# Two kinds of elementwise instruction of the attention stage moved to GpSimd

## The chip, the cores and the metric

One core of one Trainium2 chip. The time is the device time of one execution in microseconds (us), the median of three runs. Engines are called as in the profile: PE (TensorE matmul), PEld (TensorE weight load), DVE (VectorE), ACT (ScalarE), POOL (GpSimd), SP (SyncE, which issues most of the transfers here).

## What is computed

Three layers, one after another, all in float32; batch 4, 448 tokens, 12 heads of 64, model width 768:

```
attn  = sigmoid(q @ k.T / 8 - log(448)) @ v                  # per head
h     = relu(x @ w_in)                                       # 768 -> 1024, u and v are its halves
gated = u * (w_spatial @ layernorm(v) + b_spatial)
x     = gated @ w_out                                        # 512 -> 768
theta = x @ w_theta                                          # 768 -> 768
u     = x + w_tok_r @ (x * cos(theta)) + w_tok_i @ (x * sin(theta))
out   = u + relu(u @ w_ch)
```

The weights arrive as 64-bit floats and are brought to float32 on the chip.

## The kernel before

Most products are made of three passes: each operand is split into a high part (rounded to the 32-bit form that TensorE takes in one pass, `F32R`) and a low part (operand minus high part), and PE adds up high x high, high x low and low x high. So each operand needs one copy, which makes the high part, and one subtraction, which makes the low part. Both lie on DVE and ACT, beside PE.

The change touches the first of the stages, attention together with the product by `w_in`. The 48 heads (4 x 12) are worked as 24 pairs, numbered n = 0 to 23, and the pairs as 12 rounds of two. Its order is written by hand for PE, ACT, DVE and SP (`tc.manual_schedule`); POOL isn't on that list, so a planner places its instructions. A round r does this:

- `end_scores(nxt)`: scores of the 64 last tokens of the next round's pairs (tile `pse`), and their sigmoid on ACT.
- `begin_pieces(1)`, `end_pieces()`: steps of the weight pipeline, described below.
- `begin_attend` and `attend(cur)`: the products with v of this round's pairs (tile `psa`); ACT copies each result out of PSUM as the high part of `X` and DVE subtracts (`L56` in the profile, `X<-psa,X`), which frees the PSUM buffer. DVE also copies 64 columns to `XL`.
- `scores(t, g)` for both pairs of the next round, three `pss` tiles each, with a sigmoid on ACT for each (`af<-pss`).
- more steps of the weight pipeline, with `split_pair` of the two pairs of the round after that: DVE makes the high part of keys and queries (`kqh`, a cast of 128x896) and the low part (`kql`, a subtraction of 128x896).
- `uv`: products of finished heads with `w_in` (tile `psd`). There is none in rounds 0 to 2; round 3 has the first three.

All the PSUM tiles of this stage (`pse`, `psa`, `pss`, `psd`) rotate through four buffers of one tag. The third `pss` of a round takes the buffer of the round's first `psa`, the fourth that of the second: these matmuls start when DVE is through with the subtraction `X<-psa,X`.

The weight pipeline takes `w_in` in 12 pieces of 128x512 (class `Piece`), and behind them the pieces of other weights, which are only brought to float32 and stored. A piece passes through: load (SP), `low` (DVE, two instructions, L99 and L101), `high` (ACT, L106), `join` (DVE, L111, which makes the float32 value `q`), `part_high` (ACT, the high part `wih<-wq`), and `part_low` (DVE, the low part `wil<-wq,wih`). `begin_pieces` issues `part_low` of the pieces joined last time, then `join`, then `low` of the next ones, then loads; `end_pieces` issues `part_high` of the pieces just joined and `high` of the next ones. Between `join` and `part_low` of one piece there is one half of a round. From 30 to 55 us, two or three pieces pass in a round.

Pair 0 has no split: its scores are computed in plain float32. Pair 1 is split ahead of round 0, pairs 2 and 3 too, and rounds 0 to 3 split pairs 4 and 5, 6 and 7, 8 and 9, 10 and 11.

Of the kernel before, what the change touches and what calls it, by code (L numbers as in the profile page):

```python
# [14 lines left out]
ALU = mybir.AluOpType  # L15
# [35 lines left out]
def net(ctx: ExitStack, tc: tile.TileContext, kq, vd, vl, w_in, w_sp, bsp, w_out, w_th, w_tok, w_ch, out):  # L51
    nc = tc.nc
    ve, se, te = nc.vector, nc.scalar, nc.tensor

    def sub(o, a, b):
        ve.tensor_tensor(out=o, in0=a, in1=b, op=ALU.subtract)  # L56
# [4 lines left out]
    def acopy(o, a, f=AF.Copy):  # L61
        se.activation(o, a, f)  # L62
# [84 lines left out]
    wih = wi_p.tile([P, KC, DFF], F32R, name="wih")  # L147
# [29 lines left out]
    def split_pair(t):  # L177
        r = t["r"]
        hi = t["h"] = at.tile([P, 2, S], F32R, tag="kqh", name="kqh", bufs=NKQ)
        lo = t["l"] = at.tile([P, 2, S], F32R, tag="kql", name="kql", bufs=NKQ)  # L180
        ve.tensor_copy(hi, r)
        sub(lo, r, hi)

    def sigmoid(tag, ps, bufs):
        af = at.tile([P, 2, S], F32, tag=tag, name="af", bufs=bufs)
# [77 lines left out]
    class Piece:  # L263
# [18 lines left out]

        def part_high(self):
            if self.dst is None:
                acopy(wih[:, self.k, self.s], self.q)

        def part_low(self):
            if self.dst is None:
# [58 lines left out]
    with tc.manual_schedule(engines={mybir.EngineType.PE, mybir.EngineType.Activation, mybir.EngineType.DVE, mybir.EngineType.SP}):  # L347
# [4 lines left out]
        for t in rounds[0] + rounds[1]:  # L352
            load_v(t)
        split_pair(rounds[0][1])
        for g in range(3):
            scores(rounds[0][0], g)
        ae = end_scores(rounds[0])
        rounds[2] = [load_kq(4 + i) for i in range(2)]
        for t in rounds[1]:
            split_pair(t)  # L360
        for g in range(3):
            scores(rounds[0][1], g)
        for r in range(R):
# [24 lines left out]
            if aft:  # L388
                split_pair(aft[0])
# [96 lines left out]
    for i in range(2):  # L486
        t = pa.tile([P, DH], F32R, name=f"vb{i}", bufs=1)
# [452 lines left out]
```

## Time and profile before

| | us |
|---|---|
| three runs | 630.32, 624.97, 627.34; median 627.34 |
| profiled execution | 626.07 |
| its span in the trace | 624.3 |
| PE busy | 612.6 (98%) |
| PEld, DVE, ACT, POOL busy | 507.1, 415.8, 346.9, 23.8 |
| granted TensorE clock | full speed in all 40 slices |

The median of the three runs lies 1.27 us above the profiled execution. Matmuls are pipelined and their ends are modelled, so a PE that is shown as busy can still be waiting; whether it waits is read from the chain of waits and from the starts of its matmuls.

### The profile page before, as it was taken

The numbers are of one execution on the slowest core, as the hardware profiler recorded it, in microseconds if no ns is written. First come the engines' busy times: TensorE is split into PE (matmuls) and PEld (weight loads), VectorE is DVE, ScalarE is ACT, GpSimd is POOL, SyncE is SP. The second block draws the span as 40 slices with busy tenths as digits, with TensorE's granted clock in tenths as the row PEclk, the third lists the DMA queues.
The fourth block names the chain that finished last, engine by engine and source line by source line (L and its number), as shares of the span: only waits on it lengthen the run. The fifth ranks groups of instructions, "written<-read, shape, count | busy, mean of one in ns | idle before, by whom it ended". The sixth has DMA issues, their size and how long they took to land.

```text
span 624.3 us, 9178 instructions
## 1 busy us (share of the span) xinstructions
PE 612.6 (98%) x3296; PEld 507.1 (81%) x3296; DVE 415.8 (67%) x798; ACT 346.9 (56%) x588; POOL 23.8 (4%) x42
## 2 busy tenths in 40 slices
PE   6999999999999999999999999999999999899997
PEld 2455667757776688999999999999999999789996
DVE  3899576627663559794231386797776797688875
ACT  5799466564555425274336486666567566362540
POOL 0000000000000100100000000101101101000000
PEclk9999999999999999999999999999999999999999
DMA  8787588857864685865767612464183123354603
GB/s 308 239 266 233 187 237 277 271 170 250 291 212 144 203 287 180 245 207 181 220 198 230 161 39 65 89 215 114 56 247 92 50 102 126 113 191 134 224 29 134
DMA packets 82675, 112.63 MB, mean 180 GB/s; under 512 B 27842, under 2 KB 69188, under 8 KB 82628
## 3 DMA queue, kind: packets, MB, share of 16 engines
q1 hardware_dynamic: 74820, 99.18, 50.6%
q10 hardware_dynamic: 7808, 12.85, 5.9%
q8 instruction: 26, 0.43, 0.3%
q14 instruction: 21, 0.17, 0.1%
HBM read 68.06 MB, written 32.93 MB: 162 GB/s over the span
## 4 chain that ended last, share of the span: by engine, by line
PE 79%; DVE 11%; DMA 4%; ACT 3%; issue 2%; SPq 0%; POOL 0%; ACTq 0%; POOLq 0%; DVEq 0%
PE psa L224 7%; PE pss L199 6%; PE psd L65 3%; PE psd L243 3%; PE ppo L66 3%; PE ppo L67 3%; PE ppo L65 3%; PE psd L66 3%; PE psd L67 3%; PE psd L245 3%; PE psd L244 3%; PE pt L638 3%; PE pt L639 3%; PE pt L637 3%; PE py L678 3%; PE py L679 3%
## 5 line engine op out<-in xcount | busy, mean ns | idle before, releaser
L186 ACT ACTIVATE af<-pss,bias 128x896 f32<-128x896 f32 x72 | 66.1, 1020 | 2.8 <-PE pss L199 2.8
L637 PE MATMUL pt<-thh,XT 128*128 128x384 f32 x168 | 56.9, 338 | 0.3 <-DVE r L644 0.3
L638 PE MATMUL pt<-thl,XT 128*128 128x384 f32 x168 | 56.9, 338 | 0.0
L224 PE MATMUL psa<-af,vr 128*64 128x448 f32 x288 | 56.8, 543 | 0.0
L639 PE MATMUL pt<-thh,XT 128*128 128x384 f32 x168 | 56.8, 338 | 0.0
L224 PEld LDWEIGHTS psa<-af,vr 128*64 128x64 f32 x288 | 19.6, 137 | 36.3 <-issue 35.2
L62 ACT ACTIVATE ev<-psd 128x448 f32<-128x448 f32 (+1 forms) x30 | 17.0, 568 | 52.5 <-PE psd L67 26.0
L111 DVE SCALAR_TENSOR_TENSOR wq<-wraw,wq 128x384 int32<-128x384 int32 (+2 forms) x51 | 28.7, 594 | 23.7 <-ACT wraw L106 23.6
L65 PE MATMUL psd<-X,wih 128*128 128x448 f32 x96 | 35.6, 371 | 0.0
L106 ACT ACTIVATE wraw<-wraw 128x384 f32<-128x384 f32 (+2 forms) x51 | 29.6, 604 | 10.7 <-DVE wq L99 7.4
L66 PE MATMUL ppo<-g,wbh 128*128 128x448 f32 x96 | 35.2, 366 | 0.0
L67 PE MATMUL ppo<-g,wbl 128*128 128x448 f32 x96 | 35.1, 366 | 0.0
L65 PE MATMUL ppo<-g,wbh 128*128 128x448 f32 x96 | 35.1, 366 | 0.0
L67 PE MATMUL psd<-X,wil 128*128 128x448 f32 x96 | 35.1, 365 | 0.0
L66 PE MATMUL psd<-X,wih 128*128 128x448 f32 x96 | 35.1, 365 | 0.0
L56 DVE TENSOR_TENSOR X<-psa,X 128x448 fp32r<-128x448 f32 x24 | 15.0, 624 | 27.8 <-ACT X L62 27.8
L648 ACT ACTIVATE m<-r 128x384 f32<-128x384 f32 x28 | 14.6, 520 | 32.5 <-DVE r L646 32.5
L637 PEld LDWEIGHTS pt<-thh,XT 128*128 128x128 f32 x168 | 31.5, 188 | 1.1 <-DVE r L644 0.7
L638 PEld LDWEIGHTS pt<-thl,XT 128*128 128x128 f32 x168 | 31.6, 188 | 0.4
L101 DVE SCALAR_TENSOR_TENSOR wq<-wraw,wq 128x384 int32<-128x384 int32 (+2 forms) x51 | 30.6, 600 | 1.8
L639 PEld LDWEIGHTS pt<-thh,XT 128*128 128x128 f32 x168 | 31.5, 188 | 0.0
L62 ACT ACTIVATE xr<-xp 128x768 uint16<-128x768 uint16 x28 | 28.4, 1066 | 0.5 <-ACT x L62 0.5
(287 smaller groups left out, 1583.9 us busy)
## 6 DMA issues: line engine op xcount, KB each, us to landing
kqr<-in_kq SPq DMA_DIRECT2D x24, 448.0 KB, 4.6
wraw<-in_w_in SPq DMA_DIRECT2D x12, 512.0 KB, 5.3
x_d<-x ACTq DMA_DIRECT2D x24, 224.0 KB, 3.3
xb<-x_d SPq DMA_DIRECT2D x4, 1344.0 KB, 7.7
xp<-xa SPq DMA_DIRECT2D x56, 96.0 KB, 2.5
y_d<-y SPq DMA_DIRECT2D x24, 224.0 KB, 2.1
out_t<-o SPq DMA_DIRECT2D x24, 224.0 KB, 2.0
vr<-in_vd SPq DMA_DIRECT2D x24, 192.0 KB, 4.5
```

Of the source, the lines that this page charges most:

```text
L62: se.activation(o, a, f)
L65: te.matmul(ps, wh, xh, start=first, stop=False)
L66: te.matmul(ps, wh, xl, start=False, stop=False)
L67: te.matmul(ps, wl, xh, start=False, stop=last)
L101: ve.scalar_tensor_tensor(out=self.q, in0=self.hi, scalar=-(2 ** 31), in1=self.q, op0=ALU.bitwise_and, op1=ALU.bitwise_or)
L106: se.activation(self.lo.bitcast(F32), self.hi.bitcast(F32), AF.Copy, scale=2.0 ** -112)
L186: se.activation(af, ps[:, :, :S], AF.Sigmoid, bias=bias, scale=1.0 / math.sqrt(D))
L199: te.matmul(ps[:, j, :S], t[w][a, 0, c], t[x][a, 1, :], start=n == 0, stop=n == 2)
L224: te.matmul(ps[a, :S], t["v"][:, 2 * c + j, :], t["a"][c][:, j, :], start=False, stop=c == 2)
L637: te.matmul(o, t[:, k, 0, :], thh[:, k, hs], start=k == 0, stop=False)
L638: te.matmul(o, t[:, k, 0, :], thl[:, k, hs], start=False, stop=False)
L639: te.matmul(o, t[:, k, 1, :], thh[:, k, hs], start=False, stop=k == KC - 1)
```

## The change

Two instructions go to another engine. Nothing else differs; operands, tiles and sizes stay the same.

- `split_pair`: the subtraction that makes the low part of keys and queries is issued on POOL for even n up to 10, which are pairs 2, 4, 6, 8 and 10. For odd n, and from pair 12 on, it stays on DVE.
- `part_high`: the copy that makes the high part of a piece of `w_in` is issued on POOL rather than ACT. That is all 12 pieces.

```
@@ split_pair
         ve.tensor_copy(hi, r)
-        sub(lo, r, hi)
+        (ve if t["n"] % 2 or t["n"] > 10 else nc.gpsimd).tensor_tensor(out=lo, in0=r, in1=hi, op=ALU.subtract)
@@ Piece
         def part_high(self):
             if self.dst is None:
-                acopy(wih[:, self.k, self.s], self.q)
+                nc.gpsimd.tensor_copy(wih[:, self.k, self.s], self.q)
```

## Rows read from the trace of the kernel before

**Rows 1.** Busy time by stretch; us from the start, then each engine's.
```profile
20.00:40.00 20.00, 20.00 (x142) 10.31 (x144) 18.14 (x31) 18.68 (x26) 0.00 (x0) 1.00 0.74 227
40.00:60.00 20.00, 19.80 (x135) 11.00 (x132) 18.57 (x34) 18.28 (x26) 0.00 (x0) 1.00 0.79 261
60.00:80.00 20.00, 20.00 (x119) 13.47 (x119) 12.89 (x25) 11.14 (x19) 0.00 (x0) 1.00 0.56 175
```

**Rows 2.** Chain that ended last, 28 to 58 us: start, length, what.
```profile
31.72 0.64 DVE X L56
...
53.28 0.69 ACT wraw L106
53.98 0.44 ACT X L62
...
54.44 0.64 DVE X L56
...
55.12 2.88 PE pss L199 x24
57.99 0.43 PE psd L243
```

**Rows 3.** Timeline of PE: start, length, instruction, count, [idle before <-who ended it].
```profile
46.96 1.87 PE L217 MATMUL psa<-af,vends 64*64 64x448 f32 x8
...
55.12 0.47 PE L199 MATMUL pss<-kqh 64*128 64x448 f32 x2 [0.20 <-DVE X L56]
```

**Rows 4.** Timeline of DVE, 29 to 60 us.
```profile
29.19 0.69 DVE L101 SCALAR_TENSOR_TENSOR wq<-wraw,wq 128x512 int32<-128x512 int32 x1
30.52 0.62 DVE L56 TENSOR_TENSOR X<-psa,X 128x448 fp32r<-128x448 f32 x1 [0.64 <-ACT X L62]
31.72 0.62 DVE L56 TENSOR_TENSOR X<-psa,X 128x448 fp32r<-128x448 f32 x1 [0.31 <-ACT X L62]
...
37.11 1.09 DVE L56 TENSOR_TENSOR kql<-kqr,kqh 128x896 fp32r<-128x896 f32 x1
38.12 0.68 DVE L56 TENSOR_TENSOR wil<-wq,wih 128x512 fp32r<-128x512 f32 x1
...
47.24 1.09 DVE L56 TENSOR_TENSOR kql<-kqr,kqh 128x896 fp32r<-128x896 f32 x1
48.25 0.62 DVE L181 CAST kqh<-kqr 128x896 fp32r<-128x896 f32 x1
49.91 1.28 DVE L56 TENSOR_TENSOR wil<-wq,wih 128x512 fp32r<-128x512 f32 x2
```

**Rows 5.** Timeline of ACT, 18 to 60 us: the copies that move.
```profile
26.18 1.18 ACT L62 ACTIVATE wih<-wq 128x512 fp32r<-128x512 f32 x2
28.85 0.63 ACT L62 ACTIVATE wih<-wq 128x512 fp32r<-128x512 f32 x1
37.36 0.67 ACT L62 ACTIVATE wih<-wq 128x512 fp32r<-128x512 f32 x1
...
51.83 0.63 ACT L62 ACTIVATE wih<-wq 128x512 fp32r<-128x512 f32 x1 [0.63 <-DVE wq L111]
```

**Rows 6.** POOL and DVE side by side, near 500 and 527 us.
```profile
499.86 1.28 POOL L744 TENSOR_TENSOR wq<-wq 128x192 f32<-128x192 f32 x2 [8.87 <-DVE wcl L56]
500.59 0.96 DVE L627 TENSOR_TENSOR r<-xr,r 128x384 f32<-128x384 f32 x1 [0.60 <-ACT r L649]
501.47 0.54 DVE L627 TENSOR_TENSOR m<-xr,m 128x384 f32<-128x384 f32 x1
...
527.17 0.78 DVE L643 TENSOR_SCALAR m<-m 128x384 f32<-128x384 f32 x1
```

**Rows 7.** DVE's tensor_scalar of that line with POOL idle, near 488 us.
```profile
488.24 0.36 DVE L643 TENSOR_SCALAR m<-m 128x384 f32<-128x384 f32 x1
```

**Rows 8.** POOL's groups: busy, mean ns.
```profile
L488 POOL MEMSET vb<- 64x512 f32 x2 | 1.0, 524 | 201.1 <-PE pss L199 201.1
```

**Rows 9.** Who waited for whom, 60 to 80 us: total, times, longest.
```profile
DVE X L56 <- ACT X L62: 4.9, 2, 3.6
```

More of the change, by code (lines that the diff above doesn't have):

```diff
@@ L181, in split_pair @@
         ve.tensor_copy(hi, r)
-        sub(lo, r, hi)
+        (ve if t["n"] % 2 or t["n"] > 10 else nc.gpsimd).tensor_tensor(out=lo, in0=r, in1=hi, op=ALU.subtract)
     def sigmoid(tag, ps, bufs):
@@ L284, in part_high @@
             if self.dst is None:
-                acopy(wih[:, self.k, self.s], self.q)
+                nc.gpsimd.tensor_copy(wih[:, self.k, self.s], self.q)
         def part_low(self):
```

## The prediction

> **What bounds the kernel now.** I read the busy shares by stretch first. From 20 to 60 us PE, DVE and ACT are all nearly full: of every 20 us DVE works 18.1 and 18.6, ACT 18.7 and 18.3 [rows 1]. From 60 us on, when `uv` comes in, DVE falls to 12.9 and ACT to 11.1 while PE stays full [rows 1]. So the change takes work from two engines that matter only from about 20 to 55 us, which is rounds 0 to 2 and the head of round 3.
>
> Next I read the chain of waits, because a busy PE may still be waiting. Before 31 us the chain lies on PE; from 31.72 it is on DVE (with a little ACT) as far as 54.44, where it passes through an ACT step L106, the copy of `X`, DVE's subtraction `X<-psa,X`, and then the score matmuls at 55.12 [rows 2]. From there it is PE's again. What the reader is to see: in these 23 us DVE, not PE, sets the pace, and it hands over at the subtraction that frees the PSUM buffer which the third `pss` needs. In PE's timeline that is the one visible wait for DVE: 0.20 us before the matmul at 55.12 [rows 3]. So DVE and PE are almost in step there: a faster DVE gains next to nothing, while a slower DVE delays PE from the first microsecond. After 55 us nothing that PE does waits for this, and PE is busy for 98% of the whole span, so a delay that PE has at 55.12 is carried to the end.
>
> **What the subtraction costs where it goes.** On DVE the low part of a pair takes 1.09 us by itself, but 1.01 us of the queue, from its start at 47.24 to the next start at 48.25 [rows 4]. The trace of before has no instruction of this size on POOL. The nearest is POOL's two-input arithmetic on 128x192 near 500 us: two of them in 1.28 us, 0.64 each [rows 6]. That scales by elements to 896/192 x 0.64 = 2.99 us at most.
>
> More important is what DVE does meanwhile. A two-input DVE instruction of 384 columns that starts inside the second of these POOL instructions takes 0.96 us, and its twin right behind it, with POOL idle, 0.54; a one-input `tensor_scalar` takes 0.78 us beside POOL [rows 6] and 0.36 without [rows 7]. Both lose 0.42 us, at whichever form. So a POOL instruction that reads 192 columns twice stops DVE for about 0.42 us of its 0.64. I take 0.42/192 = 2.2 ns a column: a subtraction of 896 columns stops DVE for 1.9 us. Bounds: nothing (if DVE happens to be at work that POOL doesn't stop), and the full 2.99. The middle is what the rows show. Each moved subtraction gives DVE 1.01 us and takes 1.9: net **+0.9 us of DVE time**, not a relief.
>
> **What the copy costs where it goes.** On ACT a copy of 128x512 takes 0.63 us [rows 5]. On POOL no row shows a copy. Below, its hold on DVE is nothing; above, it is that of a two-input instruction, 512 x 2.2 ns = 1.1 us. It reads one operand rather than two, so I take half, 0.55 us; that POOL writes 512 columns in 0.52 us [rows 8] speaks for that order. DVE had nothing of this work before, so each copy is **+0.55 us of DVE time**, where its neighbours on DVE are instructions that POOL stops.
>
> The Trainium skill, "GPSIMD Engine Reference", section "Performance versus the Vector engine", has a two-input add of 2048 columns at 4497 ns against 2293 on VectorE, and its section on when to use GPSIMD puts one-input work at roughly line rate and names VectorE for elementwise work: by estimate 1.97 us for the subtraction and 0.43 us for the copy. With these the sum below would be 5.3 us, so the page speaks against the change as the rows do.
>
> **What ACT gets back.** 12 copies. From 30 to 55 us ACT's step that releases the late `X` is L106 at 53.28, which stands behind DVE's L99, and the copy at 51.83 was itself waiting for DVE (0.63 us) [rows 2, 5]. Its freed time turns into longer waits for DVE. I cost the relief at nothing; at most it is the 0.20 us wait of PE [rows 3] and a second one of under 0.1 behind it.
>
> **The sum.** *Round 0.* DVE is full until 29.88 us (29.19 + 0.69) and then idle for 0.64 before the first `X` subtraction at 30.52 [rows 4]. It gets one pair (pair 4, +0.9) and three copies (two at 26.18, one at 28.85 [rows 5]: 3 x 0.55 = 1.65): 2.55 us. The 0.64 idle covers part, so the first `X` subtraction starts 1.9 late, at 32.4; with the `XL` copy it takes some 0.8 of the queue, so the second starts at 33.2 instead of 31.72: **+1.5**. *Rounds 1 and 2*, 31.72 to 54.44: pairs 6 and 8, 2 x 0.9, and five copies (37.36 to 51.83 [rows 5]), 5 x 0.55: **+4.6**. The third `pss` of round 3 thus starts about 1.5 + 4.6 = 6.1 us later, at 61.2 rather than 55.12. PE's own stalls on the way, such as the 1.87 us that the `psa` matmuls at 46.96 take [rows 3], are on a PE that has to wait for DVE anyway, and give nothing back.
>
> The other moved instructions cost nothing. Pair 2 is split before 16 us with the first PE use at about 20. Pair 10 and the last four copies (0.9 + 4 x 0.55 = 3.1 us) fall after 57 us, where DVE is idle 7.1 of 20 us [rows 1] and waits 4.9 us for `X` [rows 9]. Nothing stands behind them on POOL until its memset after 201 us [rows 8]; no transfer is moved.
>
> One new wait: `wil` on DVE now needs POOL's copy, and behind `wil` stand all the later pieces and the next `X`. Between the `wil` at 38.12 and the next at 43.7 or 49.91 there is half a round, and two copies and a subtraction (1.1 + 1.9 us) fit. If the planner puts the subtraction first, `wil` at 49.91 [rows 4] waits up to half a microsecond; that is inside the range.
>
> Against the profiled execution, 626.07 + 6.1 = 632.2. The median lies 1.27 above it: **633.4 us**, +1.0%.
>
> **Rivals.** *Not slower: POOL works beside DVE.* Then each pair gives DVE 1.01 us back, and PE's last wait, 0.3 us with its successor, goes; what is late next is the sigmoid on ACT, which the change doesn't touch. 626.9 us. It needs DVE and POOL to overlap, against both rows of group 6. Decided at the `X` subtraction of 54.44: earlier or later.
> *Only the subtractions hold DVE*, because a copy reads one operand. Round 0 then adds 0.9 against 0.64 idle and the second `X` is in time; rounds 1 and 2 add 1.8: 629.1 us. No row speaks against it; the `tensor_scalar` in rows 6 and 7, one-input on DVE's side, was held all the same.
> *The hold is dearer*: a copy as dear per column as a subtraction (1.1 us). Round 0: 0.9 + 3.3 - 0.64 - 0.34 = 3.2; rounds 1 and 2: 1.8 + 5.5 = 7.3; 10.5 in all, 637.8 us. The same happens if the hold lasts for all of POOL's 0.64 rather than 0.42. The Trainium skill, "SBUF — State Buffer", section "Who interferes with whom", states that the loser of the pair of ports is blocked for the whole instruction. The 0.42 of 0.64 speaks for part of it, though DVE started some 0.1 us into the second POOL instruction.
>
> **How the numbers follow.** About 1% is what a measurement of this kernel can tell from no change. Chances: forecast 0.52, with its own range 632 to 636 (copies at 0.45 to 0.8 us); no hold 0.12; subtractions only 0.14; dearer 0.22. The 1% line is at 633.6, inside the forecast: half of it, 0.26, falls on either side. Slower by over 1%: 0.26 + 0.22 = 0.48. Within 1%: 0.26 + 0.12 + 0.14, less 0.02 = 0.50. Faster 0.02: nothing in the stretch is worth 6 us. Range 626.5 to 639.
>
> **What would show it.** On POOL, five subtractions of about 2 us and twelve copies of 0.6 to 0.8 us before 80 us; DVE instructions of 20 to 60 us lengthened by 0.5 to 1.9 us each when beside them; the matmuls at 55.12 now near 61, their wait for `X<-psa,X` much above 0.20; from there to the end the same length as before. I am wrong if DVE's instructions keep their lengths there, or if PE's delay at round 3 is made up or grows later on.

## The result, and the profile after

The changed kernel takes 631.10 us against 627.46 (medians of 12 runs each): ratio 1.0067, 95% interval 1.0046 to 1.0089, which is 2.9 to 5.6 us slower; the quotient of the two medians, 1.0058, lies inside. The forecast was slower by 6.1 us, 633.4 us. The measured time is inside the whole range (626.5 to 639) but below the range that the forecast gave its own case (632 to 636), and as near to the 629.1 us of the rival by which only the subtractions hold DVE. So the time alone doesn't decide between these two; the traces and experiments do. The profiled execution took 631.99 us, its span is 630.1; it lies 0.9 us above its median, while the one of before lay 1.4 below, so the two traces differ by more (5.8 us of span) than the medians (3.6).

Where both traces are compared I count from the second `X` subtraction of round 0 (20.53 us before [rows 4 show the ones after it], 20.27 after), because the first loads land at slightly different times. DVE before (start, length, instruction, count, idle before and what ended it), and below it PE before:

```profile
20.53 0.62 DVE L56 TENSOR_TENSOR X<-psa,X 128x448 fp32r<-128x448 f32 x1 [1.25 <-ACT X L62]
...
22.54 0.42 DVE L99 TENSOR_SCALAR wq<-wraw 128x512 int32<-128x512 uint32 x1
...
23.60 0.62 DVE L181 CAST kqh<-kqr 128x896 fp32r<-128x896 f32 x1
...
25.92 1.09 DVE L56 TENSOR_TENSOR kql<-kqr,kqh 128x896 fp32r<-128x896 f32 x1
26.93 1.29 DVE L56 TENSOR_TENSOR wil<-wq,wih 128x512 fp32r<-128x512 f32 x2
```

```profile
57.92 0.50 PE L243 MATMUL psd<-wih,X 128*128 128x512 f32 x1
```

From the second `X` subtraction of round 0 to the first of round 3 it is 33.91 us before (to 54.44 [rows 2]) and 38.28 after: **+4.4**. To the first product by `w_in` (57.92 before) it is 37.39 and 43.14: **+5.7**. From that product to the end it is 566.4 and 566.7 us: no sign that anything is made up or added there, though this stretch scatters by some 6 us between executions (see the experiments).

The stretches of the changed kernel (columns as in rows 1: after the two of the stretch, PE, PEld, DVE, ACT, POOL busy, then the granted clock, DMA share, GB/s):

```profile
20.00:40.00 20.00, 20.00 (x144) 10.03 (x142) 18.24 (x25) 15.64 (x20) 7.83 (x6) 1.00 0.65 211
40.00:60.00 20.00, 16.23 (x104) 8.87 (x102) 18.34 (x30) 12.60 (x18) 5.52 (x5) 0.90 0.75 233
60.00:80.00 20.00, 20.00 (x106) 14.44 (x106) 15.65 (x23) 10.00 (x14) 5.73 (x5) 0.93 0.50 157
```

Against [rows 1], ACT has three to six us less to do in each stretch to 60 us, and DVE is as busy as before although an instruction a round was taken from it. PE has lost 3.6 us between 40 and 60.

DVE in the changed kernel (same columns):

```profile
20.27 0.62 DVE L56 TENSOR_TENSOR X<-psa,X 128x448 fp32r<-128x448 f32 x1 [0.33 <-ACT X L62]
...
22.27 0.83 DVE L99 TENSOR_SCALAR wq<-wraw 128x512 int32<-128x512 uint32 x1
23.14 0.98 DVE L101 SCALAR_TENSOR_TENSOR wq<-wraw,wq 128x512 int32<-128x512 int32 x1
24.05 1.15 DVE L181 CAST kqh<-kqr 128x896 fp32r<-128x896 f32 x2
25.23 2.87 DVE L182 TENSOR_TENSOR kql<-kqr,kqh 128x896 fp32r<-128x896 f32 x1
28.02 1.28 DVE L56 TENSOR_TENSOR wil<-wq,wih 128x512 fp32r<-128x512 f32 x2
...
30.28 0.98 DVE L101 SCALAR_TENSOR_TENSOR wq<-wraw,wq 128x512 int32<-128x512 int32 x1
31.45 0.62 DVE L56 TENSOR_TENSOR X<-psa,X 128x448 fp32r<-128x448 f32 x1 [0.20 <-ACT X L62]
...
35.35 0.43 DVE L99 TENSOR_SCALAR wq<-wraw 128x512 int32<-128x512 uint32 x1 [1.02 <-DMA wraw<-in_w_in]
...
58.55 0.62 DVE L56 TENSOR_TENSOR X<-psa,X 128x448 fp32r<-128x448 f32 x1 [0.48 <-ACT X L62]
```

What the reader is to see: the subtraction of the odd pair, which stayed on DVE, takes 2.87 us rather than 1.09 [rows 4]. L99 at 22.27 takes 0.83 rather than 0.42, and L101 at 23.14 and 30.28 0.98 rather than 0.69 [rows 4]. And there is a wait for a load of `w_in`, which the kernel before didn't have. POOL in the changed kernel, first the subtraction of pair 2, then the instructions of this stretch:

```profile
12.75 2.08 POOL L182 TENSOR_TENSOR kql<-kqr,kqh 128x896 fp32r<-128x896 f32 x1 [11.86 <-DVE kqh L181]
...
24.80 2.36 POOL L182 TENSOR_TENSOR kql<-kqr,kqh 128x896 fp32r<-128x896 f32 x1 [1.21 <-PE pse L207]
29.97 0.74 POOL L285 CAST wih<-wq 128x512 fp32r<-128x512 f32 x1 [2.82 <-DVE wq L111]
34.40 0.61 POOL L285 CAST wih<-wq 128x512 fp32r<-128x512 f32 x1 [3.69 <-DMA wraw<-in_w_in]
```

The subtraction at 24.80 ends at 27.16; DVE's own, issued at 25.23, ends at 28.10, its usual 1.09 us after 27.01. So DVE stood until 0.15 us before POOL was done. The copy at 34.40 ran while DVE was idle: 0.61 us is its own length.

PE at the head of round 3 (same columns):

```profile
59.23 0.66 PE L199 MATMUL pss<-kqh 64*128 64x448 f32 x2 [1.93 <-DVE X L56]
59.68 0.58 PE L199 MATMUL pss<-kql,kqh 64*128 64x448 f32 x2
...
63.41 0.50 PE L243 MATMUL psd<-wih,X 128*128 128x512 f32 x1
```

The wait of 0.20 us for `X<-psa,X` [rows 3] has become 1.93. Then the matmuls take 0.58 us rather than about 0.37: the granted clock has fallen (0.90 and 0.93 in these stretches, against 1.00 before), so part of the time is at the lower of the two levels, 1.2 instead of 2.4 GHz. It is there from 45.6 to 49.2 (granted clock 0.53) and from 59.2 to 62.9 (0.54), behind waits of PE of 1.84 and 1.93 us. The third to sixth `pss` of round 3 with what follows take 4.2 us (59.23 to 63.41) rather than 2.8 (55.12 [rows 3] to 57.92): that is the step from +4.4 to +5.7.

The chain of waits shows the new load wait (start, length, what):

```profile
25.23 2.88 DVE kql L182
28.11 0.02 SPq L169
...
28.54 0.02 SPq L90
...
28.58 6.75 DMA wraw<-in_w_in
...
35.35 0.44 DVE wq L99
```

SP issues the loads of keys and queries (L169), which wait until a buffer of `kqr` is free, that is until a low part has been made from it, and behind them on the same queue the piece of `w_in` (L90). In the changed kernel the odd pair's subtraction ends late, so the piece is issued at 28.58. In the timeline of SP of the kernel before the same piece is issued at 27.50 and no DVE instruction waits:

```profile
25.41 1.99 SPq L169 DMA_DIRECT2D kqr<-in_kq  x2
27.50 0.38 SPq L90 DMA_DIRECT2D wraw<-in_w_in  x1
```

### The profile page after: what moved, and what is told of

It reads as the page before. It is cut to its first block, busy times and chain, and to the rows that moved or that the text cites. A ratio compares the mean times of both kernels' runs of the same rounds, so it can differ in the third digit from the quotient of the medians.

```text
span 630.1 us, 9187 instructions
## 1 busy us (share of the span) xinstructions
PE 615.4 (98%) x3296; PEld 509.6 (81%) x3296; DVE 421.2 (67%) x793; ACT 340.5 (54%) x576; POOL 45.6 (7%) x59
## 4 chain that ended last, share of the span: by engine, by line
PE 64%; DVE 14%; DMA 13%; ACT 4%; issue 3%; SPq 1%; POOL 1%; DVEq 0%; ACTq 0%; POOLq 0%
PE psa L224 7%; PE pss L199 5%; PE pt L638 3%; PE pt L639 3%; PE pt L637 3%; PE py L678 3%; PE py L679 3%; PE py L680 3%; DMA v<-v_d 2%; PE psd L65 2%; PE psd L243 2%; DMA wraw<-in_w_in 2%; PE ppo L65 2%; PE ppo L67 2%; PE ppo L66 2%
## 5 line engine op out<-in xcount | busy, mean ns | idle before, releaser
L111 DVE SCALAR_TENSOR_TENSOR wq<-wraw,wq 128x384 int32<-128x384 int32 (+2 forms) x51 | 28.7, 594 | 25.9 <-ACT wraw L106 25.8
L744 POOL TENSOR_TENSOR wq<-wq 128x192 f32<-128x192 f32 x24 | 16.6, 691 | 249.5 <-DMA wq<-f_ch 217.2
L101 DVE SCALAR_TENSOR_TENSOR wq<-wraw,wq 128x384 int32<-128x384 int32 (+2 forms) x51 | 32.6, 639 | 1.8
L637 PEld LDWEIGHTS pt<-thh,XT 128*128 128x128 f32 x168 | 31.5, 188 | 1.3 <-DVE r L644 0.9
L199 PE MATMUL pss<-kqh 64*128 64x448 f32 x138 | 28.6, 411 | 3.8 <-DVE X L56 3.8
```

The source lines that it names most:

```text
L101: ve.scalar_tensor_tensor(out=self.q, in0=self.hi, scalar=-(2 ** 31), in1=self.q, op0=ALU.bitwise_and, op1=ALU.bitwise_or)
L111: ve.scalar_tensor_tensor(out=self.q, in0=self.lo, scalar=3, in1=self.q, op0=ALU.logical_shift_left, op1=ALU.bitwise_or)
L199: te.matmul(ps[:, j, :S], t[w][a, 0, c], t[x][a, 1, :], start=n == 0, stop=n == 2)
L637: te.matmul(o, t[:, k, 0, :], thh[:, k, hs], start=k == 0, stop=False)
```

## The experiments

All are measured beside the kernel before on the same chip, ratios with their 95% intervals. "X of round 3" is the distance defined above, 33.91 us before and 38.28 with the change; it came out within 0.1 us of 33.91 in three kernels that differ from the kernel before only behind it or in writes of POOL, so it is a fine measure of this stretch. The whole span isn't: from the first product by `w_in` to the end the profiled executions took between 565.5 and 571.4 us, without relation to the edit.

**1. Only the subtractions.** The copy is put back on ACT:

```
-                nc.gpsimd.tensor_copy(wih[:, self.k, self.s], self.q)
+                acopy(wih[:, self.k, self.s], self.q)
```

> Only the five subtractions go to POOL; the copies stay on ACT. Theory (POOL's reads stop DVE): the DVE subtraction of the odd pair behind each lasts about 2.87 us rather than 1.09, so each pair costs DVE 1.78 - 1.01 = 0.8 us net; the X subtraction at the head of round 3, at 54.44 before and 58.55 with the whole change, comes at about 55.5 to 56.5, and the ratio is 1.002 to 1.004. Rival (what costs is that the copies arrive late or hold DVE, and the subtractions are relief): the X subtraction is not later than 54.5 and the ratio is 0.998 to 1.001.

Ratio 1.0037 (1.0017 to 1.0057); X of round 3 at 37.49, +3.6, though only 1 to 2 was expected. DVE's odd subtractions take 2.87 or 2.88 us, as expected; the rest is waits for pieces of `w_in`, 1.08, 0.37 and 0.38. One of them:

```profile
22.46 0.43 DVE L99 TENSOR_SCALAR wq<-wraw 128x512 int32<-128x512 uint32 x1 [1.08 <-DMA wraw<-in_w_in]
```

So the hold of the subtractions is shown, and they cost more than their hold, through the loads.

**2. Only the copies.** The subtraction is put back on DVE:

```
-        (ve if t["n"] % 2 or t["n"] > 10 else nc.gpsimd).tensor_tensor(out=lo, in0=r, in1=hi, op=ALU.subtract)
+        sub(lo, r, hi)
```

> Only the twelve copies of w_in go to POOL; the subtractions stay on DVE. Theory (POOL's reads stop DVE): L99 or L101 beside a copy is longer by 0.3 to 0.4 us, eight copies before 55 us add about 2.8 us less the 0.64 us of idle time in round 0, so the X subtraction of round 3 comes at 56 to 57 and the ratio is 1.002 to 1.004. Rival (a copy with one input doesn't hold DVE): 54.0 to 54.5, ratio 1.000 or a little under, since ACT has less to do.

Ratio 1.0044 (1.0020 to 1.0067), which is 1.3 to 4.2 us; X of round 3 at 35.53, +1.6, at the lower end of what was expected. PE waits for it where it waited 0.20 before:

```profile
55.66 0.47 PE L199 MATMUL pss<-kqh 64*128 64x448 f32 x2 [1.83 <-DVE X L56]
```

No load is waited for here. A one-input copy holds DVE as well; the rival that it doesn't is out.

**3. Only what falls behind 57 us.**

```
-        sub(lo, r, hi)
+        (nc.gpsimd if t["n"] == 10 else ve).tensor_tensor(out=lo, in0=r, in1=hi, op=ALU.subtract)
...
-                acopy(wih[:, self.k, self.s], self.q)
+                (nc.gpsimd.tensor_copy if self.s.start == 0 and self.k >= 2 else acopy)(wih[:, self.k, self.s], self.q)
```

> Only what falls behind 57 us goes to POOL: pair 10 and the last four pieces of w_in, where DVE has idle time. Theory (the price is paid only where DVE sets the pace): DVE's instructions beside POOL are longer there too, but PE doesn't wait; ratio 0.999 to 1.001, X subtraction of round 3 at 54.4. Rival (POOL's slower copies delay the products by w_in, or any hold is carried to the end): slower by about a third of the change's cost, ratio 1.002 or more.

Ratio 0.9998 (0.9975 to 1.0021), X of round 3 at 33.87, PE's wait there 0.20 as before. DVE's instructions beside POOL are longer here too (L99 at 57.50 takes 0.83 us, L101 at 58.37 0.98). So the same hold costs nothing that can be measured where DVE doesn't set the pace.

**4. More buffers for keys and queries.** The whole change, with

```
-        r = t["r"] = at.tile([P, 2, S], F32, tag="kqr", name="kqr", bufs=4)
+        r = t["r"] = at.tile([P, 2, S], F32, tag="kqr", name="kqr", bufs=6)
```

> The whole change, with six buffers in place of four for the loaded keys and queries, so that no load of them, nor the piece of w_in queued behind it on SP, waits for a subtraction. Theory (most of the cost is DVE held by POOL; the late load is an addition): DVE's two waits for a piece of w_in (1.02 and 0.34 us) go, the X subtraction of round 3 comes at about 57.2 rather than 58.55, the ratio falls from 1.0067 to about 1.004 to 1.005. Rival (the late loads are the cause): back to 54.5, ratio 1.000 to 1.001. Other rival (the wait only filled time that DVE would have waited anyway): no difference to the change, 1.006 to 1.007.

DVE's waits for `w_in` are gone and X of round 3 is at 37.43, 0.85 us earlier than with the change. The time isn't: 1.0081 (1.0053 to 1.0108), in 6 runs. The expected gain of 1 to 2 us didn't show, and the interval reaches to the change's own ratio and beyond, so this settles only that the late load isn't the main cause. In its profiled execution PE waited 0.99 and 2.62 us and then ran slow score matmuls (0.58 us) too; the granted clock was 0.997 or lower in all 6 executions.

**5. The same work, for nobody.** The kernel before, with POOL's instructions added and their results unused:

```
+    scr = at.tile([P, 2, S], F32, name="scr", bufs=1)
+    scr2 = at.tile([P, DH], F32, name="scr2", bufs=1)
...
         sub(lo, r, hi)
+        t["n"] in (2, 4, 6, 8, 10) and nc.gpsimd.tensor_tensor(out=scr, in0=hi.bitcast(F32), in1=hi.bitcast(F32), op=ALU.subtract)
...
                 acopy(wih[:, self.k, self.s], self.q)
+                nc.gpsimd.tensor_copy(scr2, self.q)
```

> The kernel before, with the same POOL instructions added for nobody: beside each of the five DVE subtractions a subtraction of 128x896 and beside each of the twelve ACT copies a copy of 128x512, written to tiles that nothing reads. Theory (the price is that POOL's reads stop DVE): no relief, so DVE pays 5 x about 1.8 and 0.3 for each copy; the X subtraction of round 3 comes 5 to 7 us later than before when both are counted from the second X subtraction of round 0, more than with the change itself (4.4), ratio 1.007 to 1.011. Rival (the price is that low and high parts come late from POOL): nobody waits for these results, ratio 0.999 to 1.001.

Ratio 1.0114 (1.0082 to 1.0145), X of round 3 at 40.47, +6.6. DVE does what it did before, and one instruction beside each POOL subtraction is 1.5 us longer; L99 and L101 are longer beside the copies, as in the change, and one piece of `w_in` is waited for (0.69 us, in round 0). DVE, then POOL, of this kernel:

```profile
24.69 1.09 DVE L56 TENSOR_TENSOR kql<-kqr,kqh 128x896 fp32r<-128x896 f32 x1
25.70 2.10 DVE L181 CAST kqh<-kqr 128x896 fp32r<-128x896 f32 x1
```

```profile
24.74 2.58 POOL L183 TENSOR_TENSOR scr<-kqh 128x896 f32<-128x896 f32 x1 [1.63 <-DVE kqh L181]
```

Here it is the cast that stands (2.10 rather than 0.62 us [rows 4]); the subtraction that was already running when POOL started is not lengthened, and POOL's own is (2.58, against 2.08 at 12.75 in the changed kernel). The rival, that results from POOL come late, is out as the cause: nobody waits for these.

**6 and 7. POOL that only writes.** Two memsets of 128x896 behind the split of each even pair up to 10. In the first form DVE read one element of the tile ahead of each of the two (in the cuts `tick` takes that element, and `scr` is a list that holds the tile):

```
         sub(lo, r, hi)
+        [(ve.tensor_copy(tick, s[0:1, 0:1]), nc.gpsimd.memset(s, 0.0)) for s in (2 * scr if t["n"] in (2, 4, 6, 8, 10) else ())]
```

> The kernel before, with two POOL memsets of 128x896 (about 1 us each, no reads) behind the cast of each even pair up to 10, into a tile of which DVE reads one element ahead of each (ten added DVE instructions of under 0.1 us). Theory (it is POOL's reads that stop DVE's second read): DVE's subtractions beside a memset keep 1.09 us and the time stays within 0.999 to 1.002; copies or casts of one input on DVE may be held. Rival (any POOL instruction of that length stops DVE): the subtraction beside it takes about 2 to 3 us, X subtraction of round 3 3 us or more later, ratio 1.004 or more.

1.0059 (1.0037 to 1.0081), but not for the reason asked about: the second read has to wait for the first memset, so DVE stood 1.1 us in each pair by the edit itself. Its instructions had their usual lengths. Once more, with a single read ahead of both:

```
+        [(ve.tensor_copy(tick, s[0:1, 0:1]), nc.gpsimd.memset(s, 0.0), nc.gpsimd.memset(s, 1.0)) for s in (scr if t["n"] in (2, 4, 6, 8, 10) else ())]
```

> The run with writes only once more, with DVE's one-element read ahead of both memsets rather than between them, so that DVE doesn't wait for the first. Theory (it is POOL's reads that stop DVE's two-input instructions): DVE's instructions beside the memsets keep their lengths (1.09 and about 0.63 us), X subtraction of round 3 not over 0.6 us later than before counted from the second of round 0, ratio 0.999 to 1.002. Rival (any work on POOL stops DVE): 1.5 us longer beside each pair of memsets, ratio 1.004 or more.

0.9996 (0.9975 to 1.0016), X of round 3 at 33.93. POOL, then DVE, of this kernel:

```profile
12.58 2.17 POOL L183 MEMSET scr<- 128x896 f32 x2 [10.91 <-DVE scr L183]
...
24.07 2.17 POOL L183 MEMSET scr<- 128x896 f32 x2 [9.32 <-DVE scr L183]
```

```profile
14.10 0.93 DVE L99 TENSOR_SCALAR wq<-wraw 128x512 int32<-128x512 uint32 x1
...
23.95 0.60 DVE L181 CAST kqh<-kqr 128x896 fp32r<-128x896 f32 x1
24.58 1.09 DVE L56 TENSOR_TENSOR kql<-kqr,kqh 128x896 fp32r<-128x896 f32 x1
```

At 24.07 POOL was as long at work as in a subtraction, and DVE's two-input subtraction beside it kept its 1.09 us; the cast, 0.60 us, had been issued before the memsets. So it takes more than a busy POOL to stop DVE's two-input instructions; what the subtractions and copies do and a memset doesn't is to read SBUF. For DVE's one-input instructions this doesn't hold: the `tensor_scalar` issued at 14.10, while the memsets of pair 2 ran (to 14.75), took 0.93 us rather than 0.42. It is the only one-input instruction that was issued beside a memset here, and it lies before round 0, where it delays nothing.

**8 and 9. A lighter DVE.** One piece of `w_in` fewer is loaded in round 1, so that all later pieces come one step later; first in the kernel before, then in the change:

```
-LOADS = ((1, 0), (2, 0), (2, 0)) + 8 * ((2, 2),)
+LOADS = ((1, 0), (1, 0), (2, 0)) + 8 * ((2, 2),)
```

> The kernel before with one piece of w_in fewer loaded in round 1 (all later pieces one step later), which takes about 2.2 us of DVE work out of rounds 1 and 2; PE's order is the same. Theory (DVE and PE are in step at round 3, so a faster DVE gains next to nothing): X subtraction of round 3 up to 2 us earlier, PE's wait of 0.20 there gone, ratio 0.998 to 1.001. Rival (DVE sets the time before, too): 2 us gained, ratio 0.997 or less.

> The change with the same lighter load of DVE. Theory (with the change DVE is the bound in rounds 1 and 2, so what is taken from it comes back whole): X subtraction of round 3 about 2 to 2.5 us earlier than with the change (58.55 to about 56.2), ratio 1.002 to 1.004. Rival (the cost is POOL's lateness or PE's clock, not DVE's time): 1.006 to 1.007 as with the change.

In the change: ratio 1.0019 (1.0001 to 1.0036), X of round 3 at 36.29, 2.0 us earlier than with the change, and the first product by `w_in` 3.4 earlier, since in this execution the clock stayed up. As the theory had it: of the 2.2 us or so of work taken from DVE, 2.0 come back.

In the kernel before: 0.9965 (0.9951 to 0.9980), 2.2 us faster, which is the rival's figure and not the theory's. X of round 3 comes 1.2 us earlier, PE waits for nothing there, and the first product by `w_in` comes at 36.70 instead of 37.39: the trace shows 0.7 us of gain, and the measured times show more. The 0.7 is all that PE lost to waits at the head of round 3: its six `pss` there take 4.51 us from the first to the product by `w_in` in the kernel before (53.41 to 57.92) and 3.83 here.

**10 to 12. Where that gain is from.** The same kernel a second time; one with the piece caught up in round 2, `((1, 0), (1, 0), (3, 0)) + 8 * ((2, 2),)`; and one with the piece taken from round 3 instead, `((1, 0), (2, 0), (2, 0), (2, 1)) + 7 * ((2, 2),)`.

> The kernel before with one piece fewer in round 1, a second time, on the chip of these runs. If its gain is real: 0.995 to 0.998 again. If it was chance: 0.999 to 1.001; 0.7 us of it (0.999) is what the trace showed up to the first product by w_in.

> The kernel before with one piece fewer loaded in round 1 and one more in round 2, so that all later pieces are where they were. Theory (the gain of the run with one piece later comes from DVE's lighter load up to round 3): the third pss of round 3 without a wait, as there, and the same gain, ratio 0.996 to 0.998. Rival (it comes from the later pieces lying one step later): 0.999 to 1.001. If the piece fewer only moves DVE's work into round 3's head, X subtraction as before and 1.000.

> The kernel before with one piece fewer in round 3 rather than round 1: rounds 0 to 2 as before, all later pieces one step later. Theory (lighter load of DVE before 55 us is what gains): ratio 0.999 to 1.001, PE's wait of 0.20 at round 3 still there. Rival (later pieces one step later are what gains): 0.996 to 0.998.

Again 0.9971 (0.9949 to 0.9992), with the same 36.70 us to the first product: the gain is real, about 2 us, and this version beats both kernels. The other two gave 0.9981 (0.9955 to 1.0006) and 0.9980 (0.9957 to 1.0002), with the first product at 37.27 and 37.42, as before (37.39). The six `pss` take 4.40 and 4.55 us there, so the piece caught up in round 2 takes the 0.7 back. Neither is told apart from no change nor from the whole gain. So 0.7 us is shown to come from the lighter DVE, and where the rest is from stays open.

## Why the prediction was right, and where its sizes were off

**What bounds.** Right: rounds 1 and 2 are DVE's, and its delay is handed to PE at the third `pss` of round 3 and carried to the end (experiments 3, 5 and 9). "A faster DVE gains next to nothing" was too strong: the most it could gain at PE's wait was put at 0.3 us (0.20 and under 0.1), and it is 0.7 in the trace and about 2 in the measured times (experiments 8 and 10).

**The subtractions.** Predicted hold 1.9 us and net +0.9 a pair; DVE's odd subtraction is 1.78 longer, and the split of two pairs takes 3.97 us from the first cast to the next instruction (24.05 to 28.02) rather than 3.33 (23.60 to 26.93 before): +0.64. Three pairs: 1.9 for 2.7.

**The copies.** This is the term of the sum that was mis-sized most. Half the price per column of a two-input instruction made 0.55 us each, 4.4 for eight. Measured: L101 beside a copy is 0.29 us longer (0.98 for 0.69), five times up to round 3, and L99 once 0.41 (0.83 for 0.42), 1.9 in all; the other two, at 34.40 and one of the pair at 47.54, ran while DVE waited for a load. That is 0.24 us a copy, between the forecast's 0.55 and the rival's nothing, and the 0.29 is less than the 0.5 that the prediction named as the least that would show. A copy takes POOL 0.61 us, but it stops DVE for only part of that.

**The loads.** "No transfer is moved" was true and not enough. The loads of keys wait for the buffer that the slower subtraction frees, and the pieces of `w_in` stand behind them on SP: 1.02 + 0.34 us of new DVE waits. The step looked at what is queued on POOL and on DVE, and not at who waits on SP for a buffer that comes free later.

Together, for the change: 1.9 + 1.9 + 1.4, less the idle time in round 0 that it used up (0.64 + 0.31 before [rows 4], 0.20 after: 0.75), is 4.4, as measured. The forecast's 6.1 had 2.5 too much for the copies and 0.8 too much for the subtractions, and lacked the loads; two errors against one. That the trace's +5.7 at the first product lies so near to 6.1 is luck: 3.3 us too much stood in the sum, and 1.4 of loads and 1.4 of clock did not.

**The relief of ACT** was nothing, as predicted: its freed time became waits (ACT waited 7.5 us for DVE's L99 between 20 and 66 us).

**The clock.** Not predicted: 1.4 us in the profiled execution. By it PE's delay grew from 4.4 to 5.7 us behind the third `pss`, which the prediction had named as a sign of being wrong. In the profiled executions of experiments 1, 2 and 9, whose waits were as long (2.12, 1.83 and 2.08 us), the clock stayed up, so it isn't a fixed part of the price. It is a frequent one: the mean granted clock was 0.997 or lower in 9 of the 12 executions of the change (0.994, the lowest, in the profiled one), but in 6 of 29, 2 of 29 and 1 of 34 of the kernel before, measured beside the experiments. In the five other kernels with at least three executions of either kind, the change among them, those at 0.997 or lower were slower by 0.6 to 2.0 us on average, and the 6 of 29 of the kernel before by 3.5. Why the traces differ by more than the medians stays open.

**Rivals.** "POOL works beside DVE" is out by experiment 5 (its 626.9 us should read 627.0 by its own terms, 627.34 less 0.3), "only the subtractions hold DVE" by 2, "the hold is dearer" by the lengths above. The planner did put the copies ahead of the subtraction where both were ready, and no `wil` waited for POOL.

## What to carry to other kernels

Before moving elementwise work from VectorE or ScalarE to GpSimd, find a place in the trace where both already work side by side and compare VectorE's instruction with its twin: the difference is what a moved instruction can cost VectorE, and if that is more than the move takes from VectorE, the move is free at best where VectorE has idle time (experiment 3). Follow the buffer that the moved instruction frees, too: a load that waits for it may stand ahead of other loads on its queue. Here, where one engine sets the pace in a short stretch, moving its work a step later in the schedule did more (2 us gained) than moving work to another engine (4 lost).

## What the runs showed of the hardware

A GpSimd instruction that reads SBUF stopped VectorE instructions that were issued while it ran: two-input ones, a cast and a `tensor_scalar`, all with operands in SBUF. They were longer by 1.78 us beside a subtraction of 128x896 (2.36 us), by 0.42 beside one of 128x192 (0.64 [rows 6]), and by 0.29 to 0.41 beside a copy of 128x512 (0.74, or two in 1.77). Wherever GpSimd's end can be read off, the end of the VectorE instruction less its usual length lies 0.13 to 0.16 us before it, whatever the form, as if it had stood and then run at its usual speed. The Trainium skill, "SBUF — State Buffer", section "Who interferes with whom", has the second one blocked for the whole instruction; the traces agree for the time from VectorE's issue to those 0.13 to 0.16 us before GpSimd's end. A VectorE instruction that was already running when GpSimd's started kept its length, and GpSimd's was then the longer: 2.36 us beside a cast and 2.58 beside a subtraction, against 2.08 with none running.

Memsets of GpSimd, which only write, left VectorE's two-input subtraction at 1.09 us, but a one-input `tensor_scalar` issued beside them took 0.93 us rather than 0.42 (experiment 7, one case). A cast issued just ahead of them kept 0.60 us, and the pair of memsets then took 2.17 us; it took 1.76 where VectorE was at two-input subtractions. The Trainium skill says in the same section that a two-input instruction doesn't contend with a GpSimd instruction that only writes, and that a cast or a `tensor_scalar` can contend with GpSimd; these lengths agree with both.
